# A first batch of five tiles, and the rest of it and seven more batches as one stream of 21 pairs of 512 + 512 tokens

## The chip, the core and the metric

The kernel runs on one core of one Trainium2 chip. Its time is the device time of one execution in microseconds; the kernel before took 2269.41 us (median of 3 runs, 2268.81 to 2269.79). The core has five engines that work from queues of their own: TensorE (PE) multiplies matrices, VectorE (DVE), ScalarE (ACT) and GpSimd (POOL) work element by element, and SyncE (SP) issues transfers.

## The reference

Eight batches of 3008 tokens of 256 channels are filtered in the frequency domain along the tokens, and every token then goes through two dense layers with a gelu between them (2048 wide).

```python
X = np.fft.rfft(x, axis=1)                      # x: (8, 3008, 256)
y = np.fft.irfft(X * (filt_r + 1j * filt_i)[None], n=3008, axis=1)
h = y.reshape(8 * 3008, 256) @ w_in             # 256 -> 2048
g = h * (1.0 / (1.0 + np.exp(-1.702 * h)))
out = (g @ w_out)                               # 2048 -> 256
```

## The kernel before, in words

Every large product is made three times: an operand is split into a rounded high part and a rest ("hi" and "lo"), and TensorE adds hi·hi, hi·lo and lo·hi. The splits cost ScalarE or VectorE a copy and GpSimd or VectorE a subtraction.

The first batch goes its own way. `first_fft` transforms it, and `signal` turns it back into six tiles of tokens, five of 512 and one of 448. The loop over `turns` (lines 1120 to 1154) takes one block of 128 hidden channels of one tile at a time: `first_0` makes it (6 matmuls), `gelu` applies the activation twice on ScalarE (once for gh, once in place) and subtracts on VectorE for gl, `second_0` adds it to the tile's output (6 matmuls, one block later). The first 32 blocks alternate between tiles 0 and 1, while the weights are still split into hi and lo: `w_parts` does it in steps on ScalarE, VectorE (scalar_tensor_tensor and tensor_scalar on the tile zy_of_w_tu) and GpSimd (zy, wi_of_wi, wo_of_wo). 

The other seven batches are transformed by `fft(b)`, each while the batches before it are in the dense layers. The second batch's transform `fft(1)` has an early stage, laid between the first blocks, whose products stand in the banks that the outputs of tiles 0 and 1 use (bank_o_73 to bank_o_76); its operands are named half_of_xh and half_of_xl, and its results are split into f_buf. `backward` and `parted` are the transform's last steps.

The dense layers of these batches run over pairs of tiles: `pair_signal` loads and turns back the signal of a pair (1024 tokens, and 960 in a batch's third pair: `WIDE` says 512, 512, 480), and a cycle multiplies a pair with 256 hidden channels in seven products of combined operands, 21 matmuls, and 24 matmuls into the outputs; eight cycles make a pair, so 360 matmuls. The combined weights are prepared by `sums_of` during the first batch's loop.

The order is not the order of the code. All operations are recorded, and `Planner.plan` (lines 356 to 466) lays them out again: each gets a due time from what needs it, TensorE's in the order of a target time and the others' by due time, with a price for each kind of operation (`price`, line 269) and one shared resource for GpSimd and VectorE when they work in SBUF alone (`port`). It emits all instructions from one line, so all have line 466 in the profile. The loops give it budgets by `begin(fft, ...)`: a transform that begins at block `LEAD` is due 20 us before the loop's end, the next one begins at block `NEXT`.

Of the kernel before, what the change touches and what calls it, by code (L numbers as in the profile page):

```python
# [19 lines left out]
NH = 24  # L20
P = 128
# [3 lines left out]
NG = 16  # L25

# [89 lines left out]
def _places():  # L116
# [15 lines left out]
    for b in range(B):  # L132
        for q in range(NH):
            block = b * S + time[:, :, q]
            token.append(block.ravel() if q < NH - 1 else block[0])
    return time, freq, np.concatenate(token), sign

# [340 lines left out]
def tile_kernel(  # L478
# [284 lines left out]
    def fft(b):  # L763
# [161 lines left out]
    def inverse_1(src, ps, full, t2):  # L925

        for i in range(4):
            nc.tensor.matmul(ps[:, P * i : P * i + P], src[:, i], t2, start=i == 0, stop=True, skip_group_check=True)

    def signal(t, y):  # L930

        yield
        full, w = (4, 512) if t < 5 else (3, 448)
        for m in range(2):
            ps = held(f"bt_{t}_{m}", "f", (P, 4, P))
            for i in range(4):
                q = 4 * (4 * t + i)
                nc.tensor.transpose(ps[:, i], b_t[:, m, q : q + 4].rearrange("p c s -> p (c s)"), table["eye"])
            br = nc.tile("e", (P, 4, P), F32, f"br_0_{t}_{m}")
            (nc.vector.tensor_copy if m else nc.scalar.copy)(br, ps)  # L940
            ps = held(f"i1_0_{t}_{m}", "f", (P, 512))
            inverse_1(br, ps, full, table["t2"])
            nc.scalar.copy(y[:, 0, m, :w], ps[:, :w])
            nc.vector.tensor_tensor(y[:, 1, m, :w], ps[:, :w], y[:, 0, m, :w].bitcast(F32), ALU.subtract)
            yield

    WIDE = (512, 512, 480)

    def pair_signal(b, u, ops):

        brs, base = [], []
        for t in (2 * u, 2 * u + 1):
            br = raw(f"br_{b}_{t}")
            for j in range(2):
                n = NH * j + 4 * t
                load_in(br[64 * j : 64 * j + 64], b_of[b][n : n + 4].rearrange("n k d -> k n d"))
            brs.append(br)
        yield
        yb, y22, yt = ops["b"], ops["22"], ops["t"]
        w = WIDE[u]  # L960
        names = (f"y_{b}_{2 * u}", f"y_{b}_{2 * u + 1}")
        base = [raw(name).rearrange("p a d -> p (a d)").rearrange("p (m w) -> p m w", m=2)[:, :, :w] for name in names]
        for k, to in enumerate(base):
            at = k * (512 - w)
            for m in range(2):
                ps = held(f"i1_{b}_{2 * u + k}_{m}", shape=(P, 512))
                inverse_1(brs[k][:, :, P * m : P * m + P], ps, 4, t2_sb)
                copy = nc.vector.tensor_copy if m else nc.scalar.copy
                copy(to[:, m, at:], ps[:, : w - at])
                if k == 0 and w < 512:  # L970
                    copy(base[1][:, m, : 512 - w], ps[:, w:])
# [19 lines left out]
    def finish(pos, w, at, name):  # L991

        o = nc.tile("out", (P, 2, 512), F32, name)
        nc.scalar.copy(o[:, 0, :w], pos[0][:, :w])
        nc.vector.tensor_copy(o[:, 1, :w], pos[1][:, :w])
        nc.sync.dma_start(out[:, :, at : at + w], o[:, :, :w])

    def gelu(src, w, on, name):

        gh, gl = (nc.tile(k, (P, 512), F32R, f"{k}_{name}") for k in ("gh", "gl"))  # L1000
        nc.scalar.activation(gh[:, :w], src[:, :w], AF.Gelu_apprx_sigmoid)
        nc.scalar.activation(src[:, :w], src[:, :w], AF.Gelu_apprx_sigmoid)
        on.tensor_tensor(gl[:, :w], src[:, :w], gh[:, :w].bitcast(F32), ALU.subtract)
# [17 lines left out]
    def first_0(t, y, fc):  # L1021

        w = 512 if t < 5 else 448
# [3 lines left out]
        for n, (kc, wk, yk) in enumerate([(k, *q) for k in range(2) for q in ((0, 0), (0, 1), (1, 0))]):  # L1027
            nc.tensor.matmul(ps[:, :w], wi_sb[half][:, wk, o // 2, kc, c], y[:, yk, kc, :w], start=n == 0, stop=n == 5)
        advance(6 * (w + 32) / 2400)
        gs[t, fc] = gelu(ps, w, nc.vector, f"{t}_{fc}")  # L1030

    def second_0(t, fc):
        w = 512 if t < 5 else 448
# [4 lines left out]
        for n, (wk, gk) in enumerate(((0, 0), (1, 0), (0, 1))):  # L1038
            for m in range(2):
                nc.tensor.matmul(  # L1040
                    pos[m][:, :w], wo[:, wk, P * m : P * m + P], gp[gk][:, :w],
                    start=fc == 0 and n == 0, stop=fc == NFC - 1 and n == 2,
                )
        advance(6 * (w + 32) / 2400)
        if fc == NFC - 1:
            finish(pos, w, 512 * t, f"out_{t}")
# [38 lines left out]
    def y_tile(t):  # L1085
        return nc.tile(f"y_{t % 2}", (P, 2, 2, 512), F32R, f"y_{t}")
# [31 lines left out]
    LEAD, NEXT, TAIL, AHEAD, BLANK = 24, 86, 20.0, 4, 28  # L1118
    SPAN = 3 * CYCLES * 45 * 544 / 2400
    turns = [(i, 2 * c + k) for c in range(CYCLES) for i in range(2) for k in range(2)]  # L1120
    turns += [(i, fc) for i in range(2, 6) for fc in range(NFC)]
    sigs = {}
    for n, (i, fc) in enumerate(turns):
        if n == 10:
            split_de()
        if n == LEAD:
# [15 lines left out]
        if n >= 36 and n % 6 == 0 and (n - 36) // 6 < CYCLES:  # L1142
            sums_of((n - 36) // 6)
        if 0 < i < 5 and fc in ((9, 11, 13) if i == 1 else (1, 3, 9)):
# [4 lines left out]
        elif i == 5 and fc in (4, 7, 8, 10, 11, 13):  # L1149
# [20 lines left out]
    def product_of(ps, c, a, y, w, first):  # L1170
        wt = ring_1[c % 2]
        for n, (wk, yk) in enumerate(((0, 0), (0, 1), (1, 0))):
            nc.tensor.matmul(
                ps[:, :w], wt[:, wk, a], y[yk][:, :w], start=first and n == 0, stop=n == 2, skip_group_check=True
            )
        advance(3 * (w + 32) / 2400)

    def second_of(z, k):
# [3 lines left out]
        c, pos, gs, w, name, at = z  # L1182
# [27 lines left out]
    for c, (b, u, p) in enumerate(cycles):  # L1210
# [96 lines left out]
```

## Time and profile before

| | |
|---|---|
| median of 3 runs | 2269.41 us (2268.81 to 2269.79) |
| profiled execution, its span | 2268.1 us |
| time shown for the profiled execution beside its span | none |
| TensorE busy | 2254.7 us (99%) |
| ScalarE, VectorE, GpSimd busy | 71%, 65%, 48% |
| granted clock | 1.00 in every stretch |

The time of an execution and its span differ by about a microsecond. Matmuls overlap in the profile, so their pace is read from one start to a later one, divided by the number of matmuls between them. "xN" at the end of a row means N instructions in a row of the same kind. In the names, buffers stand for the tiles that lie in them: bank_h and bank_o are banks of PSUM.

### The profile page before, as it was taken

What the parts mean: (1) busy time and instruction counts of PE and PEld (TensorE: products, weight loads), DVE (VectorE), ACT (ScalarE), POOL (GpSimd) and SP (SyncE); (2) the same over time, 40 slices, a digit from 0 to 9 for tenths busy, and PEclk for the clock granted to TensorE, in tenths of its full rate; (3) what the DMA queues carried; (4) which work ended last, traced back from release to release, by engine and by line L of the source; (5) the groups of instructions that cost most, each with busy time, mean ns of one, the idle gap of its engine ahead of it and who ended that gap; (6) DMA issues with size and microseconds to landing.
All of it is one profiled execution on the core that took longest, in us unless ns stands there. A gap on an engine that the chain in (4) does not pass through costs nothing.

```text
span 2268.1 us, 32103 instructions
## 1 busy us (share of the span) xinstructions
PE 2254.7 (99%) x10608; PEld 1902.9 (84%) x10608; DVE 1475.6 (65%) x2326; ACT 1615.4 (71%) x2949; POOL 1087.3 (48%) x941
## 2 busy tenths in 40 slices
PE   9999999999999999999999999999999999999999
PEld 8788888888888888888888888888888888888887
DVE  5777875588657775487755887558875577643433
ACT  6766766678777777677777777767777677765665
POOL 5565544456445554366543655445644455322211
PEclk9999999999999999999999999999999999999999
DMA  6756447866697667876678756887568765555443
GB/s 203 230 174 179 134 126 244 239 213 216 208 307 210 213 205 230 281 220 205 207 245 270 228 178 215 258 267 221 191 196 281 234 214 190 193 169 163 154 156 120
DMA packets 191895, 475.45 MB, mean 210 GB/s; under 512 B 19568, under 2 KB 94832, under 8 KB 191728
## 3 DMA queue, kind: packets, MB, share of 16 engines
q1 hardware_dynamic: 191584, 473.33, 66.9%
q8 instruction: 84, 1.38, 0.2%
q14 instruction: 83, 0.68, 0.1%
q10 hardware_dynamic: 144, 0.07, 0.0%
HBM read 367.94 MB, written 105.38 MB: 209 GB/s over the span
## 4 chain that ended last, share of the span: by engine, by line
PE 87%; ACT 1%; DVE 0%; POOL 0%; issue 0%; DVEq 0%; POOLq 0%
PE bank_h L466 46%; PE bank_o L466 41%; ACT bank_h L466 0%; POOL c_buf L466 0%; DVE u_buf L466 0%; DVE big_of_x L466 0%; ACT wo_of_wo L466 0%; POOL half_of_xh L466 0%; POOL u_buf L466 0%; ACT c_all L466 0%; POOL y_a L466 0%; ACT gh_of_gh L466 0%; ACT tab_of_tab L466 0%; ACT big_of_x L466 0%; DVE c_buf L466 0%
## 5 line engine op out<-in xcount | busy, mean ns | idle before, releaser
L466 PE MATMUL bank_o<-wo_of_wo 128*128 128x512 f32 (+1 forms) x2016 | 531.3, 386 | 0.0
L466 PE MATMUL bank_o<-gh_of_gh,wo_of_wo 128*128 128x512 f32 (+2 forms) x1712 | 477.8, 387 | 0.0
L466 PEld LDWEIGHTS bank_o<-wo_of_wo 128*128 128x128 f32 x2016 | 378.3, 188 | 72.3
L466 PE MATMUL bank_h<-y_of_y,wi_of_wi 128*128 128x512 f32 (+2 forms) x1560 | 427.9, 388 | 0.1
L466 PE MATMUL bank_h<-y_a,wi_of_wi 128*128 128x512 f32 (+1 forms) x1584 | 425.3, 388 | 0.2 <-DVE big_of_x L466 0.2
L466 POOL TENSOR_TENSOR gl_of_gl<-tab_of_tab,gh_of_gh 128x512 fp32r<-128x512 f32 (+1 forms) x168 | 214.9, 1279 | 414.1 <-ACT tab_of_tab L466 284.6
L466 PEld LDWEIGHTS bank_o<-gh_of_gh,wo_of_wo 128*128 128x128 f32 x1712 | 320.4, 188 | 61.5 <-ACT gh_of_gh L466 0.4
L466 ACT ACTIVATE bank_h<-bank_h 128x512 f32<-128x512 f32 (+2 forms) x600 | 349.3, 582 | 0.2
L466 PEld LDWEIGHTS bank_h<-y_a,wi_of_wi 128*128 128x128 f32 x1584 | 294.9, 188 | 55.9 <-DVE tab_of_tab L466 0.6
L466 PEld LDWEIGHTS bank_h<-y_of_y,wi_of_wi 128*128 128x128 f32 x1560 | 290.9, 188 | 55.4 <-ACT bank_h L466 0.5
L466 ACT ACTIVATE gh_of_gh<-bank_h 128x512 fp32r<-128x512 f32 (+2 forms) x260 | 153.4, 590 | 194.6 <-PE bank_h L466 186.2
L466 DVE TENSOR_TENSOR gl_of_gl<-bank_h,gh_of_gh 128x512 fp32r<-128x512 f32 (+2 forms) x260 | 176.5, 680 | 176.3 <-ACT bank_h L466 167.6
L466 DVE TENSOR_TENSOR wo_of_wo<-bank_h,wo_of_wo 128x512 fp32r<-128x512 f32 (+2 forms) x340 | 229.4, 676 | 73.0 <-ACT bank_h L466 66.0
L466 PE MATMUL bank_o<-gl_of_gl,wo_of_wo 128*128 128x512 f32 (+2 forms) x856 | 264.1, 387 | 0.6 <-DVE gl_of_gl L466 0.6
L466 PE MATMUL bank_h<-wo_of_wo,wi_of_wi 128*128 128x512 f32 (+1 forms) x960 | 264.2, 389 | 0.4 <-DVE wi_of_al L466 0.4
L466 ACT ACTIVATE wo_of_wo<-bank_h 128x512 fp32r<-128x512 f32 (+2 forms) x340 | 198.4, 583 | 30.2 <-PE bank_o L466 11.0
L466 PEld LDWEIGHTS bank_h<-wo_of_wo,wi_of_wi 128*128 128x128 f32 x960 | 178.6, 188 | 35.1 <-DVE wi_of_al L466 0.8
L466 POOL TENSOR_TENSOR zy_of_zy<-u_buf,zy_of_zy 48x512 fp32r<-48x512 f32 x112 | 158.6, 1416 | 73.0 <-DVE zy_of_zy L466 68.5
L466 POOL TENSOR_TENSOR zy_of_zy<-c_buf,zy_of_zy 48x512 fp32r<-48x512 f32 x112 | 150.3, 1342 | 88.3 <-DVE zy_of_zy L466 74.7
L466 PEld LDWEIGHTS bank_o<-gl_of_gl,wo_of_wo 128*128 128x128 f32 x856 | 160.4, 188 | 32.7 <-DVE gl_of_gl L466 1.6
L466 DVE TENSOR_TENSOR c_all<-bank_h,c_all 48x512 f32<-48x512 f32 x224 | 153.9, 687 | 49.4 <-ACT c_all L466 45.0
L466 ACT COPY wi_of_al<-bank_h 128x512 f32<-128x512 f32 (+4 forms) x235 | 134.8, 575 | 70.7 <-PE bank_h L466 65.2
(229 smaller groups left out, 3179.6 us busy)
## 6 DMA issues: line engine op xcount, KB each, us to landing
wi_of_wi<-w SPq DMA_DIRECT2D x168, 896.0 KB, 5.1
wo_of_wo<-w SPq DMA_DIRECT2D x168, 512.0 KB, 5.9
zy_of_zy<-a_d SPq DMA_DIRECT2D x224, 192.0 KB, 4.1
a_d<-big_of_x SPq DMA_DIRECT2D x98, 256.0 KB, 4.9
f_buf<-fs SPq DMA_DIRECT2D x96, 192.0 KB, 3.5
out_dram<-out_of_f_o SPq DMA_DIRECT2D x33, 512.0 KB, 7.2
b_d<-big_of_x SPq DMA_DIRECT2D x80, 192.0 KB, 4.4
big_of_x<-in_x_dram SPq DMA_DIRECT2D x29, 512.0 KB, 6.2
```

The costliest lines, as they stand in the source:

```text
L466: getattr(getattr(self.nc, o.eng), o.call)(*map(real, o.args), **{k: real(v) for k, v in o.kw.items()})
```

## The change

The first batch's own loop has five tiles. Its last 448 tokens and the seven other batches are laid into one stream of 42 tiles of 512 tokens: `_tiles()` lists what lies in each of a tile's four slots of 128, and the half blocks (64 tokens) that end two batches share a slot. All 21 pairs are 512 + 512, so the width arguments go. The first pair's first tile takes four slots of the first batch, turned back by `turned_0`; the loads of a tile go by runs of its slots. `parted` copies on ScalarE in the second batch's transform. The parity of the first tiles' buffers is swapped, the weights' sums begin at block 32 instead of 36, `NEXT` is 70 instead of 86, and from the third cycle on the second product always accumulates on a copy of the first.

```diff
+FIRST = 5
...
+def _tiles():
+    tiles, left = [], [(0, q) for q in range(4 * FIRST, NH)]
+    for b in range(1, B):
+        last, halves = [(b, NH - 1)], sum(q == NH - 1 for _, q in left)
+        whole = [(b, q) for q in range(NH - 1)]
+        left = left + (last + whole if halves else whole + last)
+        slots = []
+        for k in left:
+            if k[1] == NH - 1 and slots and slots[-1][-1][1] == NH - 1 and len(slots[-1]) == 1:
+                slots[-1].append(k)
+            else:
+                slots.append([k])
+        tiles += [slots[4 * t : 4 * t + 4] for t in range(6)]
+        left = [k for slot in slots[24:] for k in slot]
+    return tiles
...
-                nc.vector.tensor_copy(hi, p[h])
+                (nc.scalar.copy if b == 1 else nc.vector.tensor_copy)(hi, p[h])
...
-        full, w = (4, 512) if t < 5 else (3, 448)
...
+    def turned_0(t, m):
+        ps = held(f"bt_{t}_{m}", "f", (P, 4, P))
         for i in range(4):
+            q = 4 * (4 * t + i)
+            nc.tensor.transpose(ps[:, i], b_t[:, m, q : q + 4].rearrange("p c s -> p (c s)"), table["eye"])
+        br = nc.tile("e", (P, 4, P), F32, f"br_0_{t}_{m}")
+        (nc.vector.tensor_copy if m else nc.scalar.copy)(br, ps)
+        return br
...
-    WIDE = (512, 512, 480)
...
+                of_0 = turned_0(FIRST, m) if places[k][0][0] is None else None
                 ps = held(f"i1_{b}_{2 * u + k}_{m}", shape=(P, 512))
-                inverse_1(brs[k][:, :, P * m : P * m + P], ps, 4, t2_sb)
...
+                inverse_1(ps, blocks)
+                (nc.vector.tensor_copy if m else nc.scalar.copy)(to[:, m], ps)
...
-        return nc.tile(f"y_{t % 2}", (P, 2, 2, 512), F32R, f"y_{t}")
+        return nc.tile(f"y_{(t + 1) % 2}", (P, 2, 2, 512), F32R, f"y_{t}")
...
-    LEAD, NEXT, TAIL, AHEAD, BLANK = 24, 86, 20.0, 4, 28
-    SPAN = 3 * CYCLES * 45 * 544 / 2400
+    LEAD, NEXT, TAIL, AHEAD, BLANK = 24, 70, 20.0, 4, 28
+    SPAN = 3 * CYCLES * 45 * US
...
-    turns += [(i, fc) for i in range(2, 6) for fc in range(NFC)]
+    turns += [(i, fc) for i in range(2, FIRST) for fc in range(NFC)]
...
-        if n >= 36 and n % 6 == 0 and (n - 36) // 6 < CYCLES:
-            sums_of((n - 36) // 6)
+        if n >= 32 and n % 6 == 2 and (n - 32) // 6 < CYCLES:
+            sums_of((n - 32) // 6)
...
-                if c < 2 or (u == 0 and p == 0):
-                    product_of(pb, c, 1, y21, w, True)
+                if c < 2:
+                    product_of(pb, c, 1, y21, True)
```

The change also moves what stands at the start of the first batch's loop. Two places follow, each before and after. The names: half_of_xh and half_of_xl are the early stage's operands of the second batch's transform, t_sb its table, gh and gl the two parts of a gelu, wi and wo the split weights, zy_of_w_tu the tile in which weights are split.

First place, TensorE at the early stage's last products, before: nine rows in a row, the first second-layer product (gh) comes nine rows further on.

```order
MATMUL bank_o_73<-half_of_xl_0_1_500,t_sb 128x512
MATMUL bank_o_73<-half_of_xl_0_0_460,t_sb 128x512
MATMUL bank_o_75<-half_of_xh_0_0_449,t_sb 128x512
MATMUL bank_h_70<-y_0_of_y_558,wi_0_of_wi_549 128x512
MATMUL bank_h_71<-y_0_of_y_558,wi_0_of_wi_549 128x512
MATMUL bank_h_69<-tab_of_tab,e_of_br_0_1_563 128x128 x4
MATMUL bank_h_72<-tab_of_tab,b_t 128x128 x4
MATMUL bank_o_75<-half_of_xh_0_1_467,t_sb 128x512
MATMUL bank_o_75<-half_of_xh_0_0_449,t_sb 128x512
```

All early products stand ahead of the second layer's first. TensorE after, at the last two early products (into bank_o_76):

```order
MATMUL bank_o_73<-gl_of_gl_0_637,wo_0_of_wo_593 128x512
MATMUL bank_h_71<-y_0_of_y_551,wi_0_of_wi_524 128x512 x2
MATMUL bank_o_73<-gh_of_gh_1_631,wo_0_of_wo_593 128x512 x2
MATMUL bank_o_73<-gl_of_gl_1_646,wo_0_of_wo_593 128x512
MATMUL bank_h_72<-y_0_of_y_551,wi_0_of_wi_524 128x512 x6
MATMUL bank_o_76<-half_of_xh_0_1_468,t_sb 128x512
MATMUL bank_o_76<-half_of_xh_0_0_450,t_sb 128x512
MATMUL bank_o_76<-gh_of_gh_0_617,wo_0_of_wo_593 128x512 x2
MATMUL bank_o_76<-gl_of_gl_0_637,wo_0_of_wo_593 128x512
MATMUL bank_o_76<-gh_of_gh_1_631,wo_0_of_wo_593 128x512 x2
```

They stand behind second-layer products of both tiles, and tile 1's second accumulation follows them in the same bank.

GpSimd, which makes half_of_xh by a subtraction, before:

```order
TENSOR_TENSOR half_of_xl_0_1_500<-out_of_f_o_140,half_of_xh_0_1_467 128x512
TENSOR_TENSOR c_all<-c_all,u_buf_89 96x256
TENSOR_TENSOR half_of_xl_0_1_500<-out_of_f_o_145,half_of_xl_0_0_460 128x512
TENSOR_TENSOR zy_of_w_tu<-zy_of_w_tu 128x512
TENSOR_TENSOR half_of_xh_0_1_467<-out_of_f_o_145,half_of_xh_0_0_449 128x512
TENSOR_TENSOR wi_0_of_wi_549<-zy_of_w_tu,wi_0_of_wi_549 128x512
```

There it comes ahead of the first wi. GpSimd after, from behind the second layer's first weights to that subtraction:

```order
TENSOR_TENSOR wi_0_of_wi_524<-zy_of_w_tu,wi_0_of_wi_524 128x512
TENSOR_TENSOR wo_0_of_wo_593<-zy_of_w_tu,wo_0_of_wo_593 128x2x256
TENSOR_TENSOR zy_of_w_tu<-zy_of_w_tu 128x512 x2
TENSOR_TENSOR wi_0_of_wi_524<-zy_of_w_tu,wi_0_of_wi_524 128x512
TENSOR_TENSOR wo_0_of_wo_593<-zy_of_w_tu,wo_0_of_wo_593 128x2x256
TENSOR_TENSOR zy_of_w_tu<-zy_of_w_tu 128x512
TENSOR_TENSOR half_of_xh_0_1_468<-out_of_f_o_145,half_of_xh_0_0_450 128x512
```

Seven conversions (two wi, two wo, three zy) stand ahead of it.

Second place, VectorE at the conversions, before (about the fourth block's gelu):

```order
TENSOR_TENSOR gl_of_gl_1_659<-bank_h_70,gh_of_gh_1_632 128x512
SCALAR_TENSOR_TENSOR zy_of_w_tu<-big_of_x_2_115,zy_of_w_tu 128x512
TENSOR_SCALAR zy_of_w_tu<-zy_of_w_tu 128x512 x3
SCALAR_TENSOR_TENSOR zy_of_w_tu<-big_of_x_3_117,zy_of_w_tu 128x512
TENSOR_TENSOR gl_of_gl_0_641<-bank_h_69,gh_of_gh_0_619 128x512
TENSOR_TENSOR gl_of_gl_1_659<-bank_h_71,gh_of_gh_1_632 128x512
TENSOR_SCALAR zy_of_w_tu<-zy_of_w_tu 128x512 x3
```

Two gelu subtractions come after every five or so conversion steps. VectorE after, from the gelu subtraction gl_1_646 that the TensorE rows above read:

```order
TENSOR_TENSOR gl_of_gl_1_646<-bank_h_70,gh_of_gh_1_631 128x512
SCALAR_TENSOR_TENSOR zy_of_w_tu<-big_of_x_3_117,zy_of_w_tu 128x512
TENSOR_SCALAR zy_of_w_tu<-zy_of_w_tu 128x512
SCALAR_TENSOR_TENSOR zy_of_w_tu<-big_of_x_2_115,zy_of_w_tu 128x512
TENSOR_SCALAR zy_of_w_tu<-zy_of_w_tu 128x512 x4
SCALAR_TENSOR_TENSOR zy_of_w_tu<-big_of_x_1_113,zy_of_w_tu 128x512
TENSOR_SCALAR zy_of_w_tu<-zy_of_w_tu 128x512
SCALAR_TENSOR_TENSOR zy_of_w_tu<-big_of_w_152,zy_of_w_tu 128x512
SCALAR_TENSOR_TENSOR zy_of_w_tu<-big_of_x_1_113,zy_of_w_tu 128x512
TENSOR_SCALAR zy_of_w_tu<-zy_of_w_tu 128x512
SCALAR_TENSOR_TENSOR zy_of_w_tu<-big_of_w_152,zy_of_w_tu 128x512
TENSOR_SCALAR zy_of_w_tu<-zy_of_w_tu 128x512 x4
```

No gelu subtraction stands among them; one scalar_tensor_tensor and one tensor_scalar more come before GpSimd's subtraction can, and four steps more ahead of VectorE's subtraction for f_buf from bank_o_76.

## Rows read from the trace of the kernel before

**Rows 1.** The page: span, and busy time (share of span) by engine.

```profile
span 2268.1 us, 32103 instructions
...
PE 2254.7 (99%) x10608; PEld 1902.9 (84%) x10608; DVE 1475.6 (65%) x2326; ACT 1615.4 (71%) x2949; POOL 1087.3 (48%) x941
```

**Rows 2.** Busy time by stretch: length, then each engine's microseconds, granted clock, DMA.

```profile
50.00:100.00 50.00, 47.64 (x239) 38.38 (x238) 40.78 (x68) 35.70 (x67) 28.12 (x24) 1.00 0.69 218
1000.00:1500.00 500.00, 500.00 (x2325) 422.19 (x2325) 338.80 (x528) 371.67 (x677) 253.66 (x218) 1.00 0.73 230
```

**Rows 3.** Timeline, TensorE at width 512: start, length, form, count.

```profile
701.78 1.30 PE L466 MATMUL bank_h<-wo_of_wo,wi_of_wi 128*128 128x512 f32 x5
...
706.99 0.62 PE L466 MATMUL bank_o<-gh_of_gh,wo_of_wo 128*128 128x512 f32 x2
```

**Rows 4.** Timeline, TensorE at width 480.

```profile
2204.64 1.03 PE L466 MATMUL bank_h<-y_a,wi_of_wi 128*128 128x480 f32 x4
...
2215.25 1.03 PE L466 MATMUL bank_o<-wo_of_wo 128*128 128x480 f32 x4
```

**Rows 5.** Timeline, TensorE at width 448.

```profile
330.65 1.38 PE L466 MATMUL bank_h<-y_of_y,wi_of_wi 128*128 128x448 f32 x6
...
335.51 0.77 PE L466 MATMUL bank_h<-y_of_y,wi_of_wi 128*128 128x448 f32 x3
```

**Rows 6.** TensorE's waits, 40 to 100 us: total, times, longest.

```profile
PE bank_h L466 <- ACT e_of_br L466: 1.0, 1, 1.0
...
PE bank_o L466 <- DVE gl_of_gl L466: 0.4, 1, 0.4
PE bank_o L466 <- POOL c_buf L466: 0.3, 1, 0.3
```

**Rows 7.** Groups by form, GpSimd, first 300 us: busy, mean ns | idle.

```profile
L466 POOL TENSOR_TENSOR zy_of_w_tu<-zy_of_w_tu 128x512 f32<-128x512 f32 x16 | 22.2, 1386 | 28.1 <-DVE zy_of_w_tu L466 28.1
```

**Rows 8.** Timeline, VectorE, 68 to 84 us.

```profile
69.08 0.68 DVE L466 TENSOR_TENSOR y_of_y<-bank_h,y_of_y 128x512 fp32r<-128x512 f32 x1
69.68 0.68 DVE L466 TENSOR_TENSOR gl_of_gl<-bank_h,gh_of_gh 128x512 fp32r<-128x512 f32 x1
...
75.73 1.54 DVE L466 SCALAR_TENSOR_TENSOR zy_of_w_tu<-big_of_x,zy_of_w_tu 128x512 uint32<-128x512 uint32 x1 [0.88 <-ACT zy_of_w_tu L466]
...
78.57 1.70 DVE L466 SCALAR_TENSOR_TENSOR zy_of_w_tu<-big_of_x,zy_of_w_tu 128x512 f32<-128x512 uint32 x1
```

**Rows 9.** Timeline, GpSimd, 68 to 84 us.

```profile
75.44 1.28 POOL L466 TENSOR_TENSOR wi_of_wi<-zy_of_w_tu,wi_of_wi 128x512 fp32r<-128x512 f32 x1
78.43 1.29 POOL L466 TENSOR_TENSOR wo_of_wo<-zy_of_w_tu,wo_of_wo 128x512 fp32r<-128x512 f32 x1 [1.71 <-ACT wo_of_wo L466]
```

**Rows 10.** Groups by form, VectorE, first 300 us.

```profile
L466 DVE TENSOR_SCALAR zy_of_w_tu<-zy_of_w_tu 128x512 uint32<-128x512 uint32 x32 | 16.5, 516 | 1.1
...
L466 DVE SCALAR_TENSOR_TENSOR zy_of_w_tu<-big_of_x,zy_of_w_tu 128x512 uint32<-128x512 uint32 x15 | 12.1, 808 | 1.9 <-ACT zy_of_w_tu L466 1.9
```

**Rows 11.** Tile zy_of_w_tu, VectorE, 50 to 100: least, median, most ns.

```profile
L466 DVE TENSOR_SCALAR zy_of_w_tu<-zy_of_w_tu x24: 415/427/1039, 53.6 to 99.2; 128x512 uint32<-128x512 uint32 x16, 128x512 f32<-128x512 f32 x8
```

**Rows 12.** Tile f_buf, first 100 us, ScalarE and VectorE.

```profile
L466 ACT CAST f_buf<-bank_o x2: 579/599/619, 60.7 to 64.2; 128x512 fp32r<-128x512 f32 x2
...
L466 DVE TENSOR_TENSOR f_buf<-bank_o,f_buf x2: 681/681/681, 61.3 to 65.9; 128x512 fp32r<-128x512 f32 x2
```

**Rows 13.** Busy time by stretch: end of first loop, and a steady one.

```profile
185.00:325.00 140.00, 138.81 (x647) 115.72 (x646) 117.24 (x192) 95.97 (x176) 80.85 (x72) 1.00 0.47 133
720.00:860.00 140.00, 140.00 (x639) 117.27 (x638) 110.16 (x175) 106.65 (x194) 80.08 (x72) 1.00 0.65 212
```

**Rows 14.** Groups by form, 185 to 325 us: gelu on VectorE and ScalarE.

```profile
L466 DVE TENSOR_TENSOR gl_of_gl<-bank_h,gh_of_gh 128x512 fp32r<-128x512 f32 x40 | 27.5, 690 | 8.3 <-ACT bank_h L466 7.5
...
L466 ACT ACTIVATE gh_of_gh<-bank_h 128x512 fp32r<-128x512 f32 x40 | 23.9, 597 | 26.4 <-PE bank_h L466 26.3
```

**Rows 15.** Timeline, ScalarE, the last 8 us.

```profile
2262.90 0.36 ACT L466 COPY out_of_f_o<-bank_o 128x240 f32<-128x240 f32 x1 [0.31 <-PE bank_o L466]
```

More of the change, by code (lines that the diff above doesn't have):

```diff
@@ L131, in _places @@
     token = []
[L132 to L135, printed above, removed]
+    for b, q in [(0, q) for q in range(4 * FIRST)] + [k for tile in _tiles() for slot in tile for k in slot]:
+        block = b * S + time[:, :, q]
+        token.append(block.ravel() if q < NH - 1 else block[0])
     return time, freq, np.concatenate(token), sign
+def _tiles():
[13 more added lines that the diff above has]
+    return tiles
 def _layout(a):
@@ L923, in fft, with inverse_1 @@
         b_of[b] = b_d
-    def inverse_1(src, ps, full, t2):
-        for i in range(4):
-            nc.tensor.matmul(ps[:, P * i : P * i + P], src[:, i], t2, start=i == 0, stop=True, skip_group_check=True)
+    def inverse_1(ps, blocks):
+        for n, (src, t2, at, w) in enumerate(blocks):
+            nc.tensor.matmul(ps[:, at : at + w], src, t2[:, :w], start=n == 0, stop=True, skip_group_check=True)
     def signal(t, y):
         yield
-        full, w = (4, 512) if t < 5 else (3, 448)
         for m in range(2):
[L935 to L940, printed above, removed]
+            br = turned_0(t, m)
@@ L941, in signal @@
             ps = held(f"i1_0_{t}_{m}", "f", (P, 512))
[L942 to L944 removed]
+            inverse_1(ps, [(br[:, i], table["t2"], P * i, P) for i in range(4)])
+            nc.scalar.copy(y[:, 0, m], ps)
+            nc.vector.tensor_tensor(y[:, 1, m], ps, y[:, 0, m].bitcast(F32), ALU.subtract)
             yield
[L947 removed]
+    def turned_0(t, m):
+        ps = held(f"bt_{t}_{m}", "f", (P, 4, P))
+        for i in range(4):
+            q = 4 * (4 * t + i)
[3 more added lines that the diff above has]
+        return br
@@ L966, in pair_signal @@
                 ps = held(f"i1_{b}_{2 * u + k}_{m}", shape=(P, 512))
-                inverse_1(brs[k][:, :, P * m : P * m + P], ps, 4, t2_sb)
[L968 to L971, printed above, removed]
+                blocks = []
+                for src, i, at, w, *_ in places[k]:
+                    if src is None:
+                        blocks.append((of_0[:, i], table["t2"], at, w))
+                    else:
+                        blocks.append((src[:, i, P * m : P * m + P], t2_sb, at, w))
@@ L1027, in first_0 @@
         for n, (kc, wk, yk) in enumerate([(k, *q) for k in range(2) for q in ((0, 0), (0, 1), (1, 0))]):
-            nc.tensor.matmul(ps[:, :w], wi_sb[half][:, wk, o // 2, kc, c], y[:, yk, kc, :w], start=n == 0, stop=n == 5)
-        advance(6 * (w + 32) / 2400)
-        gs[t, fc] = gelu(ps, w, nc.vector, f"{t}_{fc}")
+            nc.tensor.matmul(ps, wi_sb[half][:, wk, o // 2, kc, c], y[:, yk, kc], start=n == 0, stop=n == 5)
+        advance(6 * US)
+        gs[t, fc] = gelu(ps, nc.vector, f"{t}_{fc}")
     def second_0(t, fc):
-        w = 512 if t < 5 else 448
         if fc == 0:
@@ L1168, in temp, with product_of @@
         return nc.tile("e", (P, 512), F32, name)
[L1170 removed]
+    def product_of(ps, c, a, y, first):
         wt = ring_1[c % 2]
@@ L1173, in product_of @@
             nc.tensor.matmul(
-                ps[:, :w], wt[:, wk, a], y[yk][:, :w], start=first and n == 0, stop=n == 2, skip_group_check=True
+                ps, wt[:, wk, a], y[yk], start=first and n == 0, stop=n == 2, skip_group_check=True
             )
-        advance(3 * (w + 32) / 2400)
+        advance(3 * US)
     def second_of(z, k):
```

126 lines of the change are left out of this document (73 added, 53 removed).

## The prediction

> **What bounds the kernel now.** I read the page's busy shares first, then the busy time by stretches, then TensorE's waits, then the start times of single instructions. The reader should see in the shares that TensorE is busy for 2254.7 of 2268.1 us while VectorE stands at 65%, ScalarE at 71% and GpSimd at 48% [rows 1]. By stretches TensorE is full from the stream's start on (500.00 of 500 us) and loses time only early: 2.4 us of the 50 us from 50 on [rows 2]. There its longest waits are 1.0 us for ScalarE and 0.4 us for VectorE, and no wait for GpSimd is longer than 0.3 [rows 6]. So a change is worth what it does to the number and pace of matmuls, plus any time in which TensorE stands because a slower engine is late. The granted clock is 1.00 in all these stretches [rows 2], 2.4 GHz, the upper of its two levels, so the clock has no part in the sum. Durations come from the profiled execution of 2268.1 us; the median of the three runs is 2269.41, 1.3 above it. I add the differences to the median; the clear 0.2% stands for ±4.5 us, about what can be told from no change.
>
> **Matmuls: fewer in the first batch, wider in the stream.** The old sixth tile had 16 blocks of 12 matmuls 448 columns wide: 192 go. The third pair of each of 7 batches ran 8 cycles of 45 matmuls at 480 columns: 2520 become 512 wide. The other 14 pairs had 512 already. Pace, start to start in unbroken rows: 23 matmuls of 512 from 701.78 to 706.99, 226.5 ns each [rows 3]; 49 of 480 from 2204.64 to 2215.25, 216.5 ns [rows 4]; 24 of 448 from 330.65 to 335.51, 202.5 ns [rows 5]. Removed: 192 x 202.5 = 38.9 us. Added: 2520 x 10.0 = 25.2 us. Net -13.7 us. The gain exists because 480 columns cost more than their share: 32 columns from 448 to 480 cost 14.0 ns, the next 32 only 10.0. The bounds of the second step are 14.0 (as the first), which gives 2520 x 14.0 = 35.3 and a net of -3.6, and 10.0; I take 10.0, because both widths are measured in the same kind of product.
> The Trainium skill, page "TensorE: Matmul & The Clock Gate", section "Wait — 56ns, not 53.3ns?", gives N / 2.4 GHz plus about 2.5 ns from start to start, so 13.3 ns for 32 columns at any width; by that the change would save only about 2.7 us here, an estimate from that page. The trace disagrees with its level (226.5 ns at 512, not 215.7) and with the equal steps, so the measured paces stand.
>
> **A new wait in the first 100 us.** This is where the order decides. Before, the two matmuls of the second batch's early stage that use bank_o_76 and bank_o_75 last are issued ahead of the first blocks' second products. After, one pair of them (bank_o_76 from half_of_xh_0_1_468) stands ahead of everything else that TensorE has. It reads a half that GpSimd's subtraction makes, and in GpSimd's queue that subtraction now comes behind seven weight conversions. These wait for VectorE's conversion steps, and VectorE starts them only behind the gelu subtraction gl_1_646. TensorE needs that same gl_1_646 seven matmuls earlier, so it has 7 x 0.2265 = 1.6 us of work of its own and then stops.
> How long: from gl_1_646 to the half there are 8 GpSimd operations (the seven and itself), 7 scalar_tensor_tensor and 12 tensor_scalar on VectorE, all in SBUF. The trace shows that such operations of the two engines don't run side by side: a scalar_tensor_tensor that starts inside a GpSimd operation (75.73 inside 75.44 to 76.72; 78.57 inside 78.43 to 79.72) ends 0.55 us after it, though it needs 0.6 alone [rows 8, 9]. So I add them: 8 x 1.28 = 10.2 [rows 9]; 7 x 0.55 = 3.9; 12 x 0.30 = 3.6, the 0.30 lying between 0.34 (0.43 of duration [rows 11] less the 0.09 by which a VectorE operation overlaps the next: 0.69 long, 0.60 from start to start [rows 8]) and what remains of it behind a GpSimd operation. Together 17.7, less 1.6: TensorE stands 16.1 us. Low bound, were the two engines free of each other: GpSimd alone, 10.2 - 1.6 = 8.6. High bound, every operation at the means of the first 300 us, which hold their mutual waits already: 8 x 1.386 [rows 7] + 7 x 0.808 + 12 x 0.516 [rows 10] = 22.9, less 1.6 = 21.3. I take 16.1, since every overlapping pair in the rows is exclusive.
> Behind the stop come two matmuls and then tile 1's second accumulation in the same bank. It must wait until ScalarE's copy (0.60) and VectorE's subtraction (0.68) have emptied the bank [rows 12], and the subtraction is behind four more conversion steps of about 0.5: between 0.8 (both at once free, less 0.45 of matmul) and 3.5. I take 2.0.
> What is spared: after the stop VectorE and GpSimd are some 16 us ahead with the weights, so later waits like the 0.4 us for gl [rows 6] go: -0.4. ScalarE's 1.0 comes ahead of this place and stays.
>
> **The first batch's own loop is 16 blocks shorter.** The second batch's transform is due 20 us before the loop ends, and its budget from block 24 on falls from 72 to 56 blocks of 2.72 us, by 43.5 us. In the stretch 185 to 325 VectorE is busy 117.2 of 140 us, ScalarE 96.0, GpSimd 80.9 [rows 13]. The gelu share (27.5 us on VectorE, about twice 23.9 on ScalarE, plus a few 448-wide ones [rows 14]) follows the blocks; the rest, some 88 us on VectorE, must now fit into about 105 us together with the 31 blocks whose matmuls fit there: 88 + 31 x 0.69 = 110 by durations, or 96 by start-to-start pace (0.60 of 0.69). So VectorE is 0.91 full, GpSimd 80.9 / 105 = 0.77, ScalarE about 0.8. That is closer than in the steady stream (110.2, 106.7 and 80.1 in 140 us, TensorE without a gap [rows 13]), but still under one. Short stops of 0.3 to 1 us are likely where both peak. Bounds 0 and 9 (if the stretch is paced by VectorE's and GpSimd's shared port); I take 2.0.
>
> **Edits that I cost at nothing.** The 32 copies of 48 x 512 that move from VectorE to ScalarE are about 0.5 us each in a stretch where ScalarE has a fifth to spare; uncovered they would be part of the 9 above. The stream's joint slots add a few transfers and the first pair's borrowed tile eight transposes and a few small matmuls that the old sixth tile had too. The product pb accumulates on a copy in six more cycles: one ScalarE copy for one VectorE add. The sums of weights are started four blocks earlier; they only write DRAM. The last drain is 512 instead of 480 wide: its pieces of 0.36 us [rows 15] grow by a fifteenth, under 0.1 in all. Tile parity of y swaps two equal buffers.
>
> **Sum.** -13.7 + 16.1 + 2.0 - 0.4 + 2.0 = +6.0; 2269.4 + 6.0 = 2275.4.
>
> **Rivals.**
> First, no long stop: GpSimd and VectorE are ahead of TensorE there, so the half is ready. For it: GpSimd idles 1.71 us ahead of one conversion [rows 9], and no wait for it is longer than 0.3 [rows 6]. Against it: the conversions stand behind gl_1_646 in VectorE's own queue, and that needs TensorE's result. Time 2269.4 - 13.7 + 2.0 - 0.4 = 2257.3, faster. It decides from a stop under about 10 us: then the sum is below zero.
> Second, a half stop: the conversions partly run side by side, 8.6 + 1.0: 2269.4 - 13.7 + 9.6 - 0.4 + 2.0 = 2266.9, within 0.2%.
> Third, the shortened transform becomes the bound: 9 instead of 2.0, 2282.4. For it: VectorE's 0.91. Against it: the steady stream holds nearly such loads without a gap.
> Fourth, the width costs its columns: 14.0 ns a step as from 448 to 480, 10.1 more: 2285.5. The rows at 480 and 512 speak against it. The page of the Trainium skill named above, with its 13.3, points this way.
>
> **Chances.** Forecast 0.55, its own range 2270 to 2281; first rival 0.13, second 0.12, third 0.12, fourth 0.08. The range 2263 to 2286 leaves out the first rival and the far ends. Faster by over 0.2% (below 2264.9): 0.11 of the first rival and 0.02 of the second, 0.13. Within 0.2%: 0.18 of the forecast (the stop at 11 to 14 us), 0.10 of the second and 0.02 of the first, 0.30. Slower (above 2273.9): 0.37 and the last two, 0.57.
>
> **What would show it.** In the profile after: matmuls of 512 alone, at 226 to 227 ns, and no 480 or 448; one TensorE wait of 14 to 18 us at about 73 to 76 us for GpSimd's half_of_xh, with VectorE and GpSimd alternating through it; a second wait of about 2 us for f_buf right behind; waits of under 1 us between 180 and 310; a busy TensorE from the stream's start on. The prediction is wrong if that long wait is missing or under 9 us, if 512-wide matmuls in the third pairs cost more than the others, or if the stream itself shows new stops.

## The result, and the profile after

The changed kernel takes 2295.05 us (median of 4 runs, 2293.91 to 2297.27), the kernel before 2269.11: ratio 1.0114, 95% interval 1.0100 to 1.0129. It is slower by 26 us, where 6 were forecast, and outside the range. Its profiled span is 2292.1 us, 24.0 above that of before [rows 1].

The page's span and busy shares, after:

```profile
span 2292.1 us, 31503 instructions
...
PE 2251.4 (98%) x10416; PEld 1866.8 (81%) x10416; DVE 1483.2 (65%) x2262; ACT 1638.0 (71%) x2939; POOL 1101.0 (48%) x941
```

TensorE is busy for a little less than in [rows 1] and the span is longer, so the loss is mostly standing time. By stretch (columns as in [rows 2]), first after, then the three stretches of before that differ most:

```profile
0.00:100.00 100.00, 74.99 (x475) 64.73 (x476) 72.19 (x106) 61.34 (x120) 56.49 (x61) 0.91 0.65 203
100.00:200.00 100.00, 99.66 (x459) 82.69 (x458) 60.23 (x108) 62.78 (x117) 49.81 (x40) 1.00 0.58 182
200.00:350.00 150.00, 144.76 (x654) 116.00 (x654) 110.59 (x167) 119.92 (x214) 90.73 (x82) 0.99 0.58 163
350.00:2250.00 1900.00, 1894.45 (x8668) 1572.57 (x8667) 1226.20 (x1862) 1372.10 (x2450) 898.79 (x755) 1.00 0.70 215
```

```profile
0.00:100.00 100.00, 93.01 (x561) 80.10 (x562) 64.61 (x107) 67.52 (x133) 52.27 (x59) 1.00 0.72 224
200.00:350.00 150.00, 148.81 (x707) 126.39 (x706) 115.93 (x191) 99.44 (x185) 78.21 (x69) 1.00 0.51 148
350.00:2250.00 1900.00, 1899.35 (x8817) 1601.73 (x8817) 1221.10 (x1900) 1376.21 (x2499) 900.95 (x768) 1.00 0.69 217
```

TensorE stands 25.0 us instead of 7.0 in the first 100, 5.2 instead of 1.2 in 200 to 350, and 5.6 instead of 0.7 in the stream. That is too little: a stop hides its first 0.16 us behind a draining matmul (0.39 us long, 0.23 apart), and a slow matmul counts as work. So I also summed, over all matmuls of each profiled execution, the time from one start to the next less the pace of its width (227 ns at 512, 217 at 480, 203 at 448, about 0.11 us for a pass of the small ones; a little below zero where that pace is rounded up). What counts in this table is the difference between two rows; it carries the verdicts below:

| us beyond the matmuls' pace | 0 to 100 | 100 to 200 | 200 to 350 | from 350 |
|---|---|---|---|---|
| before | 0.4 | -1.4 | 0.7 | 7.3 |
| after | 20.3 | -0.4 | 9.8 | 15.6 |
| third pairs wide | 0.7 | -1.4 | 0.7 | 19.0 |
| short first loop | 21.0 | 1.1 | 10.6 | 6.9 |
| early splits first | 4.1 | 5.0 | 11.5 | 18.0 |
| and less product | 3.3 | 4.7 | 3.5 | 16.5 |
| spread 1.02 | 20.9 | 0.0 | 9.8 | 8.9 |
| four banks | -0.9 | 2.9 | 10.5 | 16.3 |
| both | -1.3 | 2.9 | 10.6 | 11.6 |
| both, due 22 us ahead | -1.4 | 1.8 | 10.0 | 10.7 |
| both, later start | -0.7 | 2.9 | 8.2 | 3.2 |

After less before: 19.9 + 1.0 + 9.1 + 8.3 = 38.3, and -13.7 for the columns gives 24.6 of the 24.0 us. The stops by what ended them, after, first 120 us, then 120 to 360, then the rest:

```profile
PE bank_o L486 <- POOL half_of_xh L486: 14.7, 1, 14.7
...
PE bank_o L486 <- DVE f_buf L486: 3.3, 2, 2.5
```

```profile
PE bank_h L486 <- DVE big_of_x L486: 2.5, 3, 1.9
PE bank_h L486 <- DVE c_all L486: 1.7, 4, 0.7
PE bank_h L486 <- DVE gl_of_gl L486: 0.5, 2, 0.3
```

```profile
PE bank_h L486 <- DVE wo_of_wo L486: 1.7, 5, 0.6
PE bank_h L486 <- DVE tab_of_tab L486: 1.7, 9, 0.2
PE bank_h L486 <- POOL zy_of_zy L486: 1.0, 1, 1.0
PE bank_o L486 <- POOL gl_of_gl L486: 0.9, 1, 0.9
```

The first is the forecast wait, and 2.5 us of the second are the one behind it; the others are many, short, and mostly not forecast. TensorE around the long stop (start, length, form, count, idle before and its releaser):

```profile
76.06 0.39 PE L486 MATMUL bank_o<-gl_of_gl,wo_of_wo 128*128 128x512 f32 x1
76.29 1.52 PE L486 MATMUL bank_h<-y_of_y,wi_of_wi 128*128 128x512 f32 x6
92.56 1.22 PE L486 MATMUL bank_o<-half_of_xh,t_sb 128*128 128x512 f32 x2 [14.75 <-POOL half_of_xh L486]
96.31 1.22 PE L486 MATMUL bank_o<-gh_of_gh,wo_of_wo 128*128 128x512 f32 x2 [2.53 <-DVE f_buf L486]
```

Meanwhile GpSimd and VectorE take turns; GpSimd, then VectorE from gl_1_646 on (it ends at 74.82; the row of 76.06 above reads it):

```profile
80.55 1.38 POOL L486 TENSOR_TENSOR zy_of_w_tu<-zy_of_w_tu 128x512 f32<-128x512 f32 x1 [1.63 <-DVE zy_of_w_tu L486]
82.55 1.26 POOL L486 TENSOR_TENSOR zy_of_w_tu<-zy_of_w_tu 128x512 f32<-128x512 f32 x1 [0.63 <-DVE zy_of_w_tu L486]
...
90.80 1.71 POOL L486 TENSOR_TENSOR half_of_xh<-out_of_f_o,half_of_xh 128x512 fp32r<-128x512 f32 x1
```

```profile
74.15 0.68 DVE L486 TENSOR_TENSOR gl_of_gl<-bank_h,gh_of_gh 128x512 fp32r<-128x512 f32 x1
...
76.28 3.59 DVE L486 TENSOR_SCALAR zy_of_w_tu<-zy_of_w_tu 128x512 uint32<-128x512 uint32 x4
...
80.84 1.63 DVE L486 SCALAR_TENSOR_TENSOR zy_of_w_tu<-big_of_w,zy_of_w_tu 128x512 f32<-128x512 uint32 x1
82.62 1.74 DVE L486 SCALAR_TENSOR_TENSOR zy_of_w_tu<-big_of_x,zy_of_w_tu 128x512 uint32<-128x512 uint32 x1
```

VectorE's operation of 80.84 ends 0.54 us behind GpSimd's of 80.55 (82.47 and 81.93), as in [rows 8, 9]. Of the four tensor_scalar in 3.59 us, two met an operation of GpSimd and took about 1.5 us each, and two ran while it idled, at the 0.4 of [rows 11] (least, median, most in ns):

```profile
L486 DVE TENSOR_SCALAR zy_of_w_tu<-zy_of_w_tu x4: 415/946/1517, 76.3 to 79.5; 128x512 uint32<-128x512 uint32 x3, 128x512 f32<-128x512 f32 x1
```

From the end of gl_1_646 to the end of the half (74.82 to 92.51):

```profile
74.82:92.51 17.69, 2.99 (x14) 2.12 (x12) 17.33 (x22) 7.49 (x13) 11.18 (x9) 0.73 0.65 223
```

And the clock, by stretch:

```profile
78.00:92.00 14.00, 0.00 (x0) 0.00 (x0) 13.64 (x17) 6.02 (x10) 8.83 (x7) 0.68 0.72 255
92.00:94.00 2.00, 1.22 (x2) 0.50 (x2) 2.00 (x2) 0.18 (x1) 2.00 (x2) 0.50 0.00 0
94.00:97.00 3.00, 0.69 (x2) 0.59 (x3) 2.51 (x4) 2.06 (x4) 1.67 (x3) 0.50 0.39 83
97.00:99.00 2.00, 2.00 (x6) 1.56 (x5) 1.77 (x3) 1.24 (x3) 2.00 (x2) 0.50 0.95 248
99.00:101.00 2.00, 2.00 (x8) 1.60 (x7) 1.41 (x3) 1.46 (x3) 1.03 (x2) 0.75 0.98 223
101.00:104.00 3.00, 3.00 (x15) 2.48 (x14) 1.69 (x2) 1.59 (x4) 2.84 (x2) 1.00 1.00 359
...
290.00:293.00 3.00, 3.00 (x12) 2.43 (x11) 0.90 (x2) 2.03 (x4) 2.84 (x4) 0.81 0.91 240
```

After the stop TensorE runs at 0.50, 1.2 GHz, until about 100. From 92.56 to 100.40 it starts 12 matmuls (7.8 us); 2.7 of it is their pace at full clock and 2.5 the second stop, so the clock costs about 2.6. It falls once more behind a stop of 1.9 us at 285, to 0.81 in the last row.

The engines where the second batch's transform is densest (205 to 309 us, in which the copies of `parted` lie) and in two parts of it, then these copies on ScalarE and the gelu subtraction on VectorE, 185 to 325 us as in [rows 14]:

```profile
205.00:309.00 104.00, 98.76 (x429) 77.36 (x428) 85.53 (x125) 92.07 (x164) 69.04 (x65) 0.98 0.58 153
225.00:250.00 25.00, 23.91 (x103) 19.35 (x104) 22.10 (x32) 23.43 (x43) 16.90 (x16) 1.00 0.75 207
250.00:275.00 25.00, 24.65 (x113) 19.22 (x112) 19.92 (x32) 23.88 (x44) 16.34 (x16) 1.00 0.60 171
```

```profile
L486 ACT CAST zy_of_zy<-u_buf 48x512 fp32r<-48x512 f32 x16 | 9.9, 619 | 0.9 <-POOL u_buf L486 0.6
L486 ACT CAST zy_of_zy<-c_buf 48x512 fp32r<-48x512 f32 x16 | 9.9, 616 | 0.8 <-PE bank_h L486 0.5
...
L486 DVE TENSOR_TENSOR gl_of_gl<-bank_h,gh_of_gh 128x512 fp32r<-128x512 f32 x40 | 27.5, 690 | 23.8 <-ACT bank_h L486 23.2
```

ScalarE is 0.89 full there and VectorE 0.82. VectorE waits 23.2 us for ScalarE ahead of its gelu subtractions, where it was 7.5 before [rows 14].

The stream's matmuls in a stretch of the last third pair, 48 from the first start to the second, 226.7 ns each, where before had 216.5 [rows 4]:

```profile
2210.57 0.84 PE L486 MATMUL bank_h<-y_a,wi_of_wi 128*128 128x512 f32 x3
...
2221.45 0.84 PE L486 MATMUL bank_o<-gh_of_gh,wo_of_wo 128*128 128x512 f32 x3
```

### The profile page after: what moved, and what is told of

Read it like the earlier page. It is cut to its first block, busy times and chain, and to the rows that moved or that the text cites. A ratio compares the mean times of both kernels' runs of the same rounds, so it can differ in the third digit from the quotient of the medians.

```text
span 2292.1 us, 31503 instructions
## 1 busy us (share of the span) xinstructions
PE 2251.4 (98%) x10416; PEld 1866.8 (81%) x10416; DVE 1483.2 (65%) x2262; ACT 1638.0 (71%) x2939; POOL 1101.0 (48%) x941
## 4 chain that ended last, share of the span: by engine, by line
PE 83%; DVE 2%; ACT 1%; issue 0%; POOL 0%; DMA 0%; POOLq 0%; ACTq 0%
PE bank_h L486 43%; PE bank_o L486 39%; DVE zy_of_zy L486 0%; DVE u_buf L486 0%; DVE tab_of_tab L486 0%; DVE big_of_x L486 0%; DMA wo_of_wo<-w 0%; ACT gh_of_gh L486 0%; DVE c_all L486 0%; POOL zy_of_zy L486 0%; DVE wi_of_br L486 0%; ACT c_all L486 0%; ACT bank_h L486 0%; DVE wo_of_wo L486 0%; ACT tab_of_tab L486 0%
## 5 line engine op out<-in xcount | busy, mean ns | idle before, releaser
L486 PE MATMUL bank_o<-wo_of_wo 128*128 128x512 f32 x2016 | 535.7, 390 | 0.0
L486 PE MATMUL bank_o<-gh_of_gh,wo_of_wo 128*128 128x512 f32 x1648 | 462.7, 392 | 3.3 <-DVE f_buf L486 3.3
L486 POOL TENSOR_TENSOR gl_of_gl<-tab_of_tab,gh_of_gh 128x512 fp32r<-128x512 f32 x168 | 218.1, 1298 | 497.4 <-ACT tab_of_tab L486 400.3
L486 PE MATMUL bank_h<-y_a,wi_of_wi 128*128 128x512 f32 x1584 | 431.7, 392 | 2.1 <-DVE wo_of_wo L486 1.1
L486 PE MATMUL bank_h<-y_of_y,wi_of_wi 128*128 128x512 f32 x1464 | 415.1, 393 | 3.6 <-DVE big_of_x L486 2.5
L486 ACT ACTIVATE bank_h<-bank_h 128x512 f32<-128x512 f32 x584 | 346.3, 593 | 0.3
L486 DVE TENSOR_TENSOR wo_of_wo<-bank_h,wo_of_wo 128x512 fp32r<-128x512 f32 x340 | 233.8, 688 | 80.5 <-ACT bank_h L486 68.0
L486 PE MATMUL bank_h<-wo_of_wo,wi_of_wi 128*128 128x512 f32 x960 | 268.6, 392 | 1.3 <-DVE tab_of_tab L486 0.7
L486 PE MATMUL bank_o<-gl_of_gl,wo_of_wo 128*128 128x512 f32 x824 | 263.3, 393 | 1.6 <-POOL gl_of_gl L486 0.9
L486 ACT ACTIVATE wo_of_wo<-bank_h 128x512 fp32r<-128x512 f32 x340 | 201.0, 591 | 28.9 <-PE bank_o L486 15.8
```

What stands on the lines that cost most here:

```text
L486: getattr(getattr(self.nc, o.eng), o.call)(*map(real, o.args), **{k: real(v) for k, v in o.kw.items()})
```

## Experiments: the parts of the change apart

**e1_wide**, the kernel before with wide third pairs:

```diff
-    WIDE = (512, 512, 480)
+    WIDE = (512, 512, 512)
```

> The kernel before with all third pairs 512 + 512 wide (the last 64 columns are computed and not written); the first batch's loop keeps six tiles. Theory: 2520 matmuls gain 10.0 ns, +25.2 us, and the wide pairs bring the short TensorE stops of the stream, +8: about 2302 us, with stops of 0.3 to 1.2 us at the same places of each batch and none in the first 350 us that before did not have. Rival A: the stream's stops come from the joint slots and the borrowed tile, which this kernel lacks: +25, about 2294. Rival B: no new stops, but 512 costs 14.0 ns more than 480: about 2304, with a wider spacing of the matmuls.

Measured 2306.54 us against 2269.23 (ratio 1.0165, 1.0148 to 1.0182), +37.3: 11.7 more in the stream by the table, nothing ahead of it, and the rest, 25.6, is the 25.2 for the columns. The new stops, at 715:

```profile
715.30 0.39 PE L466 MATMUL bank_h<-zy_of_zy,e_sb 128*128 128x256 f32 x1 [0.95 <-POOL zy_of_zy L466]
716.64 0.80 PE L466 MATMUL bank_o<-gl_of_gl,wo_of_wo 128*128 128x512 f32 x1 [0.96 <-POOL gl_of_gl L466]
```

The stream's loss thus comes with the width, without joint slots or a borrowed tile, and the columns cost about 10.0 ns: both rivals fall.

**e2_short**, the kernel before with the short loop (and the loop's side edits, not repeated here):

```diff
-    turns += [(i, fc) for i in range(2, 6) for fc in range(NFC)]
+    turns += [(i, fc) for i in range(2, 5) for fc in range(NFC)]
```

> The kernel before with five tiles in the first batch's loop and the side edits of that loop (parity, sums, NEXT, parted on ScalarE); tile 5's 448 tokens are left out of the computation, the stream keeps 512, 512, 480. Theory: the shortened loop alone brings the long stop near 77 us and the stops of the second batch's transform: -38.9 + 20 + 10 = -9, about 2260 us, and the stream has no new stops. Rival: the long stop comes with the joined stream: -38.9 + 1, about 2231.

Measured 2259.82 us (0.9958, 0.9943 to 0.9973), -9.4. One wait of 16.6 us for half_of_xh, 10.6 us lost in 200 to 350, and 6.9 in the stream, about as before. So the shortened loop with its side edits brings both the long stop and the transform's stops, and none of the stream's. It doesn't part the shortening from the side edits: a rival that no run tests is that the transform's stops come with `parted` on ScalarE, 19.8 us more there in the shortened time.

## Experiments: the long stop and the transform

**e3_rush** puts the early splits first:

```diff
             due = target.get(n, now + 20.0)
+            if any(k[:5] in ("xh_1_", "xl_1_") and k[5] in "01" for k in o.names):
+                due -= 60.0
```

> The changed kernel with the early stage's operand splits due 60 us earlier in the planner, so that GpSimd makes them ahead of the weight conversions. Theory: the waits of 14.7 + 2.5 us go, and with them the half clock behind them (about 3 us): -20, about 2275 us, clock 1.00 in the stretch 75 to 100. Rival: the conversions are the bottleneck themselves and TensorE then waits for weights: the gain is under 8, about 2288.

Measured 2285.97 us, 9 below the changed kernel, not 20: the long stop is gone, 16 us less in the first 100, but 5.4 come back in the next, 1.7 and 2.4 in the later stretches (by the table, whose profiled execution, 2287.61 us, is 6.3 below the other's). The longest waits, 50 to 200 us:

```profile
PE bank_o L488 <- POOL wo_of_wo L488: 2.3, 3, 1.1
PE bank_o L488 <- ACT wo_of_wo L488: 1.3, 3, 0.5
```

TensorE now waits for the second layer's weights. The rival held in part.

**e4_noproduct** adds to it:

```diff
+            if b > 1 or g == 0:
                 nc.vector.tensor_tensor(q, t, f_i, ALU.mult)
+            if b > 1:
                 nc.gpsimd.tensor_tensor(p[:, 0], p[:, 0], q[:, 1], ALU.subtract)
                 nc.gpsimd.tensor_tensor(p[:, 1], p[:, 1], q[:, 0], ALU.add)
```

> As the run with the early splits first, and the second batch's transform leaves out most of the product with the filter (one VectorE multiplication and both GpSimd operations of each of its groups), so its output is not the reference's. Theory: the stops between 170 and 310 us come from the load on VectorE and the port it shares with GpSimd: they fall from about 9.5 to under 5 us, -5 against that run, about 2270. Rival: the chain of matmul, ScalarE copy and VectorE addition through the banks sets the pace there, not the load: within 1 us of that run, about 2275.

Measured 2277.28 us, 8.7 less, 8.0 of it between 200 and 350 us. The planner lays out the shorter list anew, so the order changes with the load, and the run doesn't say which of them, or which engine's load, counts; e9 to e11 below keep the order.

**e6_banks**. In the planner, a due time is handed back from a bank's next user; the code took one bank for the four that the blocks and the transform share, so their due times hang on one chain (in the kernel before too, where it brought no long stop):

```diff
-                size = self.caps.get(t.kind, 1 if t.pool == "h" else len(self.sites[t.pool]))
+                size = self.caps.get(t.kind, 4 if t.pool == "h" else len(self.sites[t.pool]))
```

> The changed kernel with the planner's due times following the four banks that the hidden blocks and the transform share (a later user of a bank waits for the fourth one before it), where they followed a single bank. Theory: with one bank, the due times of everything up to the shortened transform are chained and lie some 30 us too early, so that the weight conversions are put ahead of the early splits; with four the conversions are due late again, the long stop, the one behind it and the half clock go, and no new waits come as in the run with early splits due 60 us earlier: -20, about 2275 us. Rival: the conversions and the transform's steps are the bottleneck there whatever the order, as the returned 9 us of that run suggest: about 2286.

Measured 2278.58 us (1.0043, 1.0028 to 1.0058), 16.5 below the changed kernel. The stretch that had the long stop:

```profile
75.00:100.00 25.00, 24.80 (x109) 20.14 (x108) 20.14 (x32) 19.11 (x36) 12.56 (x10) 1.00 0.75 230
```

It is full, at full clock, and little took the stop's place: 21.2 us go from the first 100, 3.3 come back in the next. So the stop came from an order by due times, not from work that could not be done in time. The 30 us of the expectation were not read from any run. The stretch 200 to 350 stays at 10.5.

**e9, e10, e11** keep the order of the run "due 22 us ahead" (e8_tail, below: 2270.40) and let some operations touch an eighth of their columns: GpSimd's product in the second batch's transform, ScalarE's second activation, VectorE's gl. The marks that do it:

```diff
+        def cut(n, a):
+            if n not in self.thin or not isinstance(a, (bass.AP, View)):
+                return a
+            return a[(slice(None),) * (len(a.shape) - 1) + (slice(0, a.shape[-1] // 8),)]
```

> As the run with both edits and the transform due 22 us before the loop's end, in exactly its order; GpSimd's 32 operations of the second batch's product with the filter work on an eighth of their columns (the rest of the product is left out), which takes some 18 us from GpSimd and the port that it shares with VectorE. Theory: the stops that are left between 180 and 350 us (10 us) come from that port: they fall by half or more, -5 against that run, 2265. Rival: another engine sets them: within 1.5 us, 2270.

> The same order again; ScalarE's second activation of the 48 blocks of tiles 2 to 4 works on an eighth of its columns (the low part of these blocks is wrong in the rest), some 19 us less on ScalarE. Rival to the port: ScalarE, busy for 24.0 of 25 us between 225 and 250, sets the stops: -5 or more, 2265. By the theory of the port: within 1.5 us, 2270.

> The same order again; VectorE's subtraction for gl of the 48 blocks of tiles 2 to 4, whose source is in PSUM and needs no shared port, works on an eighth of its columns (the low part is left out in the rest), some 24 us less on VectorE. If VectorE's own time sets the stops: -5 or more, 2265, and if it is the port alone: up to -3, since VectorE comes earlier to its port work, 2268; if ScalarE: within 1.5 us, 2270.

Measured 2267.27, 2267.82 and 2265.85 us: 3.1, 2.6 and 4.6 less, or 3.6, 3.0 and 5.0 when each is set against the kernel before as measured beside it (2269.18 with e8_tail, 2269.60 here). From 200 to 350 us the loss is 6.3, 8.3 and 5.8 instead of 10.0. GpSimd and ScalarE end between their two answers; VectorE comes to the edge of the 5 us that were to speak for its own time. Each gives a part of the stretch's loss and none the half, which fits stops where the three, one behind the other, have little slack left. That one of them is the bound is not shown. Nor is `parted` cleared: in the 105 us in which its copies lie there (185 to 290), thinning took ScalarE only from 91.9 to 86.3 us busy, less than the 19.8 us of the copies, and no run leaves the copies on VectorE.

## Experiments: the stream's stops, and a faster version

**e5_span**:

```diff
-                begin(fft(b + 2), SPAN)
+                begin(fft(b + 2), 1.02 * SPAN)
```

> The changed kernel with the later transforms spread over 1.02 of a batch's time in the stream (in the kernel before they were spread over 1.02 of it, because its third pairs were narrower and the span was not). Theory: the stream's short stops, 8.2 us more than before in the changed kernel and 11.7 in the run with wide third pairs, come from that lost slack in the order: -8 to -12, about 2285 us, the first 350 us as in the changed kernel. Rival: they come from the load, ScalarE and VectorE having a fifteenth more to do in every third pair: within 2 us of 2295.

Measured 2288.22 us, 6.8 less, 6.7 of it in the stream (15.6 to 8.9), nothing ahead of it. A little less than expected; the theory holds, the load is unchanged. `SPAN` always counted 24 cycles of 512; a batch took less in the kernel before (8 of them were 480 wide), so each transform was paced about a sixtieth slower than its batch (244.8 us against 720 matmuls at 226.5 ns and 360 at 216.5, 241.0); 1.02 is a little more than that.

**e7_both** joins the two, **e8_tail** sets `TAIL` to 22.0 besides:

> Both edits together: spread 1.02 and four banks in the due times. Theory: the two gains add, since they lie in different parts of the program: 2295 - 10 - 20 = 2265 us, below the kernel before. Rival: the second batch's transform, ordered anew, passes its delay on to the stream's start: the gains don't add, 2272 or more.

> As the run with both edits, and the second batch's transform due 22 instead of 20 us before the end of the first batch's loop. Theory: what is left, the stops between 170 and 350 us, comes from the load in the shortened window; a window that is 2 us shorter makes it worse by up to 3: about 2267. Rival: the stops depend on where the transform's steps fall between the blocks more than on the load; then it may be 3 us better, 2262.

Measured 2272.41 (1.0016, 1.0006 to 1.0025) and 2270.40 us (1.0006, 0.9997 to 1.0015). The gains add to 22.6 of 23.3, but both edits are smaller than I had expected: the rival's time came, its reason did not. The window that is 2 us shorter is not worse, as the load alone would have it, but 2.0 us better (the intervals overlap).

**e12_later** starts the first pair two blocks later and spreads the transforms over 1.03:

```diff
-        elif i == FIRST - 1 and fc in (4, 7, 8, 10, 11, 13):
-            if fc == 4:
+        elif i == FIRST - 1 and fc in (6, 8, 10, 11, 12, 13):
+            if fc == 6:
...
-                begin(fft(b + 2), SPAN)
+                begin(fft(b + 2), 1.03 * SPAN)
```

> As the run with both edits; the first pair's signal is begun two blocks later (blocks 6 to 13 of the last tile instead of 4 to 13), and the later transforms are spread over 1.03 of a batch's time. Theory: the stops of 1.0 us that recur once in each batch depend on where the transform's steps fall and go with another spread, -4, and the first pair's start keeps out of the transform's last steps, -2: about 2266 us, under the kernel before. Rival: both are ties to the load: 2272 as the run with both edits.

Measured 2262.28 us against 2269.60: ratio 0.9970, 0.9958 to 0.9981. It beats both kernels. The stream:

```profile
350.00:2250.00 1900.00, 1899.78 (x8724) 1583.57 (x8723) 1218.89 (x1864) 1374.83 (x2457) 896.07 (x754) 1.00 0.69 214
```

TensorE stands 0.2 us in 1900, less than in the kernel before. Against the run with both edits it is 10.1 us less, 8.4 of it in the stream and 2.4 in 200 to 350 by the table; of the two edits the run doesn't say which did it. With 8.2 us still lost in 200 to 350, the 13.7 us are not all collected.

## Why the prediction was wrong

**Columns: right.** 192 matmuls of 448 out, 2520 at 226.7 instead of 216.5 ns; e1_wide has the 25.2 without the rest of the change. By the Trainium skill ("TensorE: Matmul & The Clock Gate", section "Wait — 56ns, not 53.3ns?"), whose N / 2.4 GHz makes 13.3 ns of every 32 columns, an estimated 2.7 of the 13.7 us would have been left; the measured step decides.

**The new wait: right in place and cause, near in size.** 14.7 us for half_of_xh at 78 us where 16.1 were taken, 2.5 for f_buf where 2.0 (0.7 more for f_buf at 74). From gl_1_646 to the half it took 17.69 us, the 17.7 of the sum; that they agree so well is luck, since GpSimd was busy for 11.2 of them, not 10.2, and VectorE's part was as much smaller. TensorE read gl_1_646 1.2 us after it was ready, so it had 3.0 us of work left, not 1.6. What I had not asked is why the order had changed there: the loop's edits and the planner's one-bank chain (e2_short, e6_banks).

**The clock: wrong.** That "the clock has no part in the sum" held for before; behind the stop that I forecast it stood at 0.50, which cost 2.6 us, and behind the 1.9 us of stop at 285 it stood at 0.81. e6_banks, without the long stop, has 1.00 there.

**The first loop's shortened budget: the step that failed first.** I took 2.0 us between 0 and 9; it is 9.1 in 200 to 350 us, the third rival's price. I had worked out 0.91 for VectorE, about 0.8 for ScalarE, and read it as "still under one". Measured, it is the other way round, 0.82 and 0.89, with ScalarE at 23.4 and 23.9 of 25 us in two parts: the copies of `parted`, which I cost at nothing, were still in VectorE's sum and not in ScalarE's, where they take 19.8 us. And none of the three was full over the whole stretch. How much of it is load, whose, and how much order stays open (e9 to e11).

**The stream: the step that failed next.** I expected no new stops, and named them as a sign of being wrong; the other two pairs of a batch were 512 wide already and ran without a gap. 8.3 us came there. The steady stretch that I read as proof owed most of its quiet to a schedule with slack, which the narrower third pairs gave it (e1_wide takes it away, e5_span gives 6.7 us back): an unpriced edit, since the diff rewrites `SPAN` to the same value and leaves the line that hands it to the transforms alone.

Together: 2.6 for the clock, 7 for the budget and 8 for the stream make 18 of the 20 us by which the sum was short; the clock's second fall is within the 7.

## What to carry over

Where a planner orders the work, a constant whose value the diff leaves alone can change its meaning: look for budgets that were counted in units that the change alters. Don't take a busy share under one as cover: here ScalarE at 0.89 and VectorE at 0.82, one behind the other, went with 9.1 us lost. When an edit moves work from one engine to another, move it in the sum too. And when an order gets worse far from the edit, follow the due time back before moving single operations ahead: e6_banks won 16.5 us, e3_rush 9.1.

## What was not expected of the hardware

Behind a TensorE stop of 14.7 us the clock stood at 0.50 for some 8 us, and behind one of 1.9 us a stretch stood at 0.81. VectorE's tensor_scalar, 0.43 us alone, took about 1.5 us where it met an operation of GpSimd.
